# First slab's norm ahead, a four-tile opening for slabs 0 and 1, and a middle stage placed two places earlier

## The chip, the cores and the metric

The kernel runs on one core of one Trainium2 chip. The metric is the device time of one execution in microseconds (us), as a median of several runs. Engines are named as the profile names them: PE (TensorE, matmuls; PEld is its weight loads), DVE (VectorE), ACT (ScalarE), POOL (GpSimd) and SP (SyncE, which here only issues DMAs). ACT and POOL issue some DMAs too.

## The reference

```
x = A_x                                    # (1, 2048, 640), bf16
xn = layernorm(x)                          # over the 640 columns, eps 1e-5
s = irfft2(rfft2(xn) * (w_r + 1j * w_i))   # over rows and columns, s in bf16
g = silu((gelu(xn @ w_gate) * (xn @ w_up)) @ w_down)    # 640 -> 1536 -> 640, Gelu by its tanh form
return x + s * g
```

## The kernel before, in words

The 2048 rows are cut into 16 **slabs** of 128 rows (X[:, n1, :], 640 columns each). Two branches are worked on at once.

The feed-forward branch takes the slabs in four groups of four (g = 0 to 3). A slab is normalized in place (`norm`, L218), turned by five PE transposes or a DMA transpose into XG, and then multiplied with the weights: for each of 12 weight **tiles** of 128 columns (t), five matmuls with Wg into the PSUM bank psg and five with Wu into psu (`ffn_piece`, L832; one of the two for all four slabs, 512 columns, is a "half tile"). ACT takes the Gelu of psg (L837), DVE multiplies it with psu into UT (L839). Then the down projection follows, either plainly (`down_third`, L967) or, for groups 1 and 2, as 14 `product`s of six matmuls of 320 columns (L933) with DVE and ACT work between them (L937 copies, L947 sums, L870 and L867 Tanh and Silu, L875 leftovers of the Tanh form, L907 sums of parts).

The spectral branch is a chain of small matrix products. Its first stage writes ZDR to DRAM. The **middle stage** reads it back as B (`load_B2`, L603) and runs in steps (`s2_step`, L681): step b puts px(b) on PE (L628), then pu(b-1) (L657); DVE begins the sort of pu(b-1) (L672); ACT copies px(b) to xs (L640) and DVE multiplies that with the spectral weights W1 and W2 (L644); ACT ends the sort (L672, two copies) and, every other step, SP stores the result to UDR. px and pu take turns in the two buffers of the pool psB, so pu needs the sort of the pu before it finished. The **inverse stage** loads UDR (`load_V`), transforms slab by slab (L735, L762, with ACT copies L737 and L763), and `finish` multiplies, adds x and stores.

The order is written by hand. `back` (L1000) is the list of PE's feed-forward pieces in order, one **place** each; `plan[s]` holds what is emitted behind place s, filled by `put(s, ...)`. Each engine runs its own instructions in that order. Group 0 takes places 0 to 35 and begins, while weights still arrive, with narrower pieces: slab 0 alone on tiles 0 and 1, slab 1 alone on them, slabs 0 and 1 together (256 columns) on tiles 2 to 7, then slabs 2 and 3 together on tiles 0 to 7. Places 60 to 71 and 96 to 107 hold the products of groups 1 and 2, one or two in each; other places hold a half tile or a third of a plain down projection. The middle stage's first step stands behind place `sb` = 67 (L1111), its later ones at sb + 3, 5, 7 and so on, and everything of the inverse stage counts on from there.

Loads: SP issues x slab by slab, Wu, and later tiles of both weights (L94 to L106); ACT issues Wg's tiles 0 to 5, two tiles to a load (L231). A load with two tiles reads rows of 512 bytes. A DMA whose turn among eight semaphores is still taken waits on its issuing engine.

The opening: PE runs 21 **warm-up** matmuls of 256 columns on ones (L588). DVE takes the statistics of a slab in two halves of 320 columns (`bn_half`, L189) and joins them (`bn_join`, L195). The root is taken for slab 0 by ACT (`root_act`, L214, behind which the Gelu table is loaded, L215), for later slabs by DVE (L205, adding epsilon) and POOL (L207, a power). The order on DVE is: statistics of slab 0, first half of slab 1, second half of slab 1, join, epsilon (L205), then the norm of slab 0 in two column parts, 0 to 383 and 384 to 639 (`norm_parts`, L984). `slab_Tparts` (L988) transposes the two parts into psB and copies the first to XG by DVE, the second by ACT (L995).

Of the kernel before, what the change touches and what calls it, by code (L numbers as in the profile page):

```python
# [10 lines left out]
BF16 = mybir.dt.bfloat16  # L11
INT32 = mybir.dt.int32
ACT = mybir.ActivationFunctionType
ALU = mybir.AluOpType
P = 128
# [17 lines left out]
def kernel(  # L33
# [39 lines left out]
    with tc.manual_schedule():  # L73
        build(nc, locals())


def build(nc, env):
    consts, big, wts, work, psA, psB = (env[k] for k in ("consts", "big", "wts", "work", "psA", "psB"))
    ZDR, UDR, X, Wg, Wu, Wd, W1, W2 = (env[k] for k in ("ZDR", "UDR", "X", "Wg", "Wu", "Wd", "W1", "W2"))
    xv, outv, wgv, wuv = (env[k] for k in ("xv", "outv", "wgv", "wuv"))  # L80
    A_w_r, A_w_i, B_w_down = (env[k] for k in ("A_w_r", "A_w_i", "B_w_down"))

    def load_x(n0, n, eng=nc.sync):
        eng.dma_start(out=X[:, n0:n0 + n, :], in_=xv[:, n0:n0 + n, :])

    def load_w(k, t0, t1, eng=nc.sync):
        f0, f1 = t0 * P, t1 * P
        eng.dma_start(out=(Wg, Wu)[k][:, :, f0:f1], in_=(wgv, wuv)[k][:, :, f0:f1])

    def load_gu(t0, t1):  # L90
        for k in range(2):
            load_w(k, t0, t1)

    load_x(0, 1)  # L94
    load_x(1, 1)
    load_w(1, 0, 2)
    load_w(1, 2, 4)
    load_x(2, 1)
    load_w(1, 4, 6)
    load_x(3, 1)  # L100
    load_gu(6, 8)
    load_x(4, 4)
    load_gu(8, 12)
    load_x(8, 4)
# [32 lines left out]
    UT = consts.tile([P, NT, 512], BF16, name="UT")  # L137
# [8 lines left out]
    def slot(k, *shape):  # L146
        return XG[:, k, :].rearrange("p (a b) -> p a b", b=shape[-1])
# [25 lines left out]
    def c1(name, dt=FP32):  # L173
        return consts.tile([P, 1], dt, name=name)

    done = set()
    mva = {}
    rstd = {}
    rall = {}
    nmr = {}  # L180
    xnT = {}
# [4 lines left out]
    def bn_half(n1, k):  # L186
        if k == 0:
            st_n[n1] = work.tile([P, 2, nc.vector.BN_STATS_DIM], FP32, tag="st", bufs=3, name="st")
        nc.vector.bn_stats(out=st_n[n1][:, k, :], in_=X[:, n1, 320 * k:320 * k + 320])  # L189

    def bn_join(n1):
        g = n1 // 4
        if g not in mva:
            mva[g] = work.tile([P, 4, nc.vector.BN_AGGR_DIM], FP32, tag="mva", bufs=2, name=f"mva{g}")
        nc.vector.bn_aggr(out=mva[g][:, n1 % 4, :], in_=st_n[n1])  # L195
# [6 lines left out]
    def root(n0, n):  # L202
        m = mva[n0 // 4][:, n0 % 4:n0 % 4 + n, :]
        ve = work.tile([P, 4], FP32, tag="ve", name="ve")[:, 0:n]
        nc.vector.tensor_scalar(out=ve, in0=m[:, :, 1], scalar1=1e-5, scalar2=None, op0=ALU.add)  # L205
        r = work.tile([P, 4], FP32, tag="rst", bufs=4, name="rst")[:, 0:n]
        nc.gpsimd.tensor_tensor(out=r, in0=ve, in1=mhalf[:, 0:n], op=ALU.pow)  # L207
        rall[n0] = r
        for k in range(n):
            rstd[n0 + k] = r[:, k:k + 1]  # L210

    def root_act(n1):
        rstd[n1] = c1("rst0")
        nc.scalar.activation(out=rstd[n1], in_=mva[n1 // 4][:, n1 % 4, 1:2], func=ACT.Abs_reciprocal_sqrt, bias=eps)  # L214
        nc.scalar.activation(out=warm, in_=negpi, func=ACT.Gelu_apprx_tanh)  # L215

    def norm(n1, c0=0, c1_=D):
        nc.vector.tensor_scalar(out=X[:, n1, c0:c1_], in0=X[:, n1, c0:c1_], scalar1=mva[n1 // 4][:, n1 % 4, 0:1],  # L218
                                scalar2=rstd[n1], op0=ALU.subtract, op1=ALU.mult)
        if c1_ == D:  # L220
            done.add(("n", n1))
# [6 lines left out]
    eps = c1("eps")  # L228
    nc.vector.memset(eps, 1e-5)
    nc.scalar.activation(out=warm, in_=eps, func=ACT.Abs_reciprocal_sqrt)  # L230
    for t in (0, 2, 4):  # L231
        load_w(0, t, t + 2, nc.scalar)
    b_0, b_1 = c1("b_0"), c1("b_1")
    nc.vector.memset(b_0, 320.0)
    nc.vector.memset(b_1, 0.0)
# [92 lines left out]
    stats(0)  # L328
    bn_half(1, 0)
    root_act(0)  # L330

    def tinv_phase(h):
# [251 lines left out]
    def warm_pe(n):  # L584
        if not warm_bank:
            warm_bank.append(bank(0))
        for _ in range(n):
            nc.tensor.matmul(warm_bank[0][:, 0:256], lhsT=ones[:, 0:P], rhs=ones, start=True, stop=True)  # L588
# [230 lines left out]
    def bank(k):  # L819
        return psA.tile([P, 512], FP32, tag="gu"[k], name="ps" + "gu"[k])  # L820

    cur = {}

    ges = {}

    def ffn_piece(g, t, k, c0, c1_):
        for j in range(c0 // P, c1_ // P):
            assert ("T", 4 * g + j) in done
        ps = bank(k)[:, c0:c1_]
        WT = (Wg, Wu)[k]  # L830
        for c in range(5):
            nc.tensor.matmul(ps, lhsT=WT[:, c, t * P:(t + 1) * P], rhs=xnT[g][:, c, c0:c1_],  # L832
                             start=(c == 0), stop=(c == 4))
        flush()
        if k == 0:
            ges[t] = work.tile([P, 512], BF16, tag="ge", bufs=3, name="ge")[:, c0:c1_]
            nc.scalar.activation(out=ges[t], in_=ps, func=ACT.Gelu_apprx_tanh)  # L837
        else:
            nc.vector.tensor_tensor(out=UT[:, t, c0:c1_], in0=ps, in1=ges[t], op=ALU.mult)  # L839

    def ffn_part(g, t, h):
        for k in range(2):
            ffn_piece(g, t, k, h * 256, h * 256 + 256)

    def ffn_half(g, t, k):
        ffn_piece(g, t, k, 0, 512)
# [8 lines left out]
    def flush():  # L855
        now = put_off[:]
        del put_off[:]
        for f in now:
            f()
# [109 lines left out]
            if t == NT - 1:  # L969
                gated(g, j, k, ph)  # L970

    def ffn_slab(j, tk):
        for t, k in tk:
            ffn_piece(0, t, k, j * P, j * P + P)

    GG, UU = ((0, 0), (1, 0)), ((0, 1), (1, 1))

    def run(*items):
        for it in items:
            it[0](*it[1:])  # L980

    PARTS = ((0, 3), (3, 5))

    def norm_parts(n1):  # L984
        for a, b in PARTS:
            norm(n1, a * P, b * P)

    def slab_Tparts(n1):  # L988
        if n1 == 0:
            xnT[0] = slot(0, 5, 512)  # L990
        for (a, b), ev in zip(PARTS, (nc.vector.tensor_copy, nc.scalar.copy)):
            pt = psB.tile([P, 5, P], BF16, tag="b")
            for c in range(a, b):
                nc.tensor.transpose(out=pt[:, c, :], in_=X[:, n1, c * P:(c + 1) * P], identity=ident)  # L994
            ev(out=xnT[0][:, a:b, n1 * P:n1 * P + P], in_=pt[:, a:b, :])  # L995
        done.add(("T", n1))

    NP = 8
    STR = (1, 2)
    back = [(run, (ffn_slab, 0, GG), (norm_parts, 1), (slab_Tparts, 1), (vt_iota, 1), (ffn_slab, 0, UU),  # L1000
             (inv_consts, 0), (inv_consts, 1)),
            (run, (ffn_slab, 1, GG + UU), (stats, 2), (root, 2, 1))]
    for h in range(2):
        for t in range(0 if h else 2, NP):
            back.append((ffn_part, 0, t, h))
        if h == 0:
            back[-1] = (run, (ffn_piece, 0, NP - 1, 0, 0, 256), (slab_Tparts, 3), (ffn_piece, 0, NP - 1, 1, 0, 256))
    for g in range(4):
        for t in range(NP if g == 0 else 0, NT):
            for k in range(2):  # L1010
# [10 lines left out]
    def put(s, *item):  # L1021
        plan[s].append(item)

    put(1, inv_rest)
    put(2, norm, 2)
    put(3, bn_half, 3, 0)
    put(4, bn_half, 3, 1)
    put(4, bn_join, 3)
    put(4, root, 3, 1)
    put(4, slab_T, 2, 1)  # L1030
    put(5, norm, 3)
    for g in range(5):
        put(3 + g, ft_v, g)
        put(8 + g, ft_v, 5 + g)
# [73 lines left out]
    put(z_end, load_B2)  # L1108
    for k in range(2):
        put(TURN + k, mg_turn, k)  # L1110
    sb = 67  # L1111
    AT = (0, 3, 5, 7, 9, 11, 13, 15, 17, 19, 21)
    for b in range(len(BURSTS)):
        put(sb + AT[b], s2_step, b)
# [9 lines left out]
    for i, (n0, n) in enumerate(DG):  # L1124
        a = vs0 + 6 * i
# [3 lines left out]
        d = a + (7 if n == 3 else 4)  # L1129
# [3 lines left out]
        for k in range(n):  # L1133
            put(min(d + 8 + k, LAST), finish, n0 + k)

    warm_pe(21)
    bn_half(1, 1)
    bn_join(1)
    root(1, 1)
    norm_parts(0)  # L1140
    slab_Tparts(0)
    warm_pe(2)

    put(5, phase_const)

# [35 lines left out]
```

## Time and profile before

| what | us |
|---|---|
| three runs: median (lowest to highest) | 193.76 (193.47 to 193.83) |
| the profiled execution's own time | 193.65 |
| its span (first to last instruction) | 191.9 |
| PE busy | 186.1 |
| DVE busy | 150.9 |
| ACT busy | 131.9 |
| POOL busy | 53.9 |
| slab 0 landed; slab 1 landed | 3.10; 4.36 |
| norm of slab 0 begins; first transpose; first real matmul | 5.62; 6.05; 6.84 |
| last matmul begins | 188.44 |

All clock readings in this document count from the span's start, those of one profiled execution. Durations of matmuls are modelled ends: the distance from one start to the next tells the pace. The 1.75 us between the span and the execution's own time lie outside what the trace shows.

### The profile page before, as it was taken

The numbers are of one execution on the slowest core, as the hardware profiler recorded it, in microseconds if no ns is written. First come the engines' busy times: TensorE is split into PE (matmuls) and PEld (weight loads), VectorE is DVE, ScalarE is ACT, GpSimd is POOL, SyncE is SP. The second block draws the span as 40 slices with busy tenths as digits, with TensorE's granted clock in tenths as the row PEclk, the third lists the DMA queues.
The fourth block names the chain that finished last, engine by engine and source line by source line (L and its number), as shares of the span: only waits on it lengthen the run. The fifth ranks groups of instructions, "written<-read, shape, count | busy, mean of one in ns | idle before, by whom it ended". The sixth has DMA issues, their size and how long they took to land.

```text
span 191.9 us, 4068 instructions
## 1 busy us (share of the span) xinstructions
PE 186.1 (97%) x1453; PEld 115.6 (60%) x1469; DVE 150.9 (79%) x364; ACT 131.9 (69%) x241; POOL 53.9 (28%) x91
## 2 busy tenths in 40 slices
PE   7999999999999999999999999999999999999993
PEld 5788854677655665566543334347775555556772
DVE  6787889899799889846978677685445898888973
ACT  4658557957878778536697878634989776876622
POOL 4458768999040200000000000002030134150400
PEclk9999999999999999999999999999999999999999
DMA  6999999948889994249996444149900084778842
GB/s 164 300 329 360 370 332 170 172 99 318 178 165 191 211 300 120 78 111 230 223 108 123 106 103 103 42 107 273 266 5 0 0 117 111 152 153 213 121 174 62
DMA packets 39700, 32.43 MB, mean 169 GB/s; under 512 B 12928, under 2 KB 37760, under 8 KB 39552
## 3 DMA queue, kind: packets, MB, share of 16 engines
q1 hardware_dynamic: 35888, 27.91, 58.6%
q0 software_dynamic: 1824, 3.28, 9.4%
q10 hardware_dynamic: 1968, 0.98, 1.9%
q8 instruction: 11, 0.18, 0.4%
q14 instruction: 9, 0.07, 0.1%
HBM read 19.03 MB, written 7.88 MB: 140 GB/s over the span
## 4 chain that ended last, share of the span: by engine, by line
PE 95%; DMA 2%; DVE 1%; issue 1%; SPq 0%; ACT 0%
PE psu L832 27%; PE psg L832 27%; PE psg L967 7%; PE psg L933 7%; PE psu L967 6%; PE psu L933 5%; PE pu L657 2%; PE pd L762 2%; PE pv L735 2%; PE pz L555 2%; PE pd L573 2%; PE px L628 2%; DMA X<-in_A_x_dram 2%; PE pt L994 1%; PE pd L575 1%
## 5 line engine op out<-in xcount | busy, mean ns | idle before, releaser
L832 PE MATMUL psu<-XG,Wu 128*128 128x512 bf16 (+2 forms) x284 | 60.4, 342 | 0.5 <-issue 0.3
L832 PE MATMUL psg<-XG,Wg 128*128 128x512 bf16 (+2 forms) x280 | 60.1, 341 | 0.6
L839 DVE TENSOR_TENSOR UT<-psu,ge 128x512 bf16<-128x512 f32 (+2 forms) x58 | 34.4, 594 | 13.6 <-PE psu L832 8.1
L837 ACT ACTIVATE ge<-psg 128x512 bf16<-128x512 f32 (+2 forms) x58 | 30.3, 523 | 21.3 <-PE psg L832 20.6
L832 PEld LDWEIGHTS <-Wu 128*128 128x128 bf16 x290 | 25.9, 98 | 20.9 <-issue 3.4
L832 PEld LDWEIGHTS <-Wg 128*128 128x128 bf16 x290 | 26.5, 98 | 18.8 <-issue 0.2
L967 PEld LDWEIGHTS <-UT 128*128 128x128 bf16 x204 | 19.1, 98 | 6.9
L813 POOL DMA_DIRECT2D VY<-in_A_x_dram x12 | 10.6, 964 | 26.2 <-ACT W L737 10.5
L713 POOL COPY vr<-VY 128x128 bf16<-128x128 bf16 x2 | 0.6, 291 | 60.2 <-DMA VY<-UDR 60.2
L644 DVE TENSOR_TENSOR RZ<-xs,W 128x960 bf16<-128x960 bf16 (+2 forms) x22 | 13.3, 647 | 4.4 <-ACT xs L640 4.4
L967 PE MATMUL psg<-Wd,UT 128*128 128x320 bf16 (+1 forms) x108 | 15.7, 290 | 0.0
L578 ACT CAST RZ<-pd 128x660 bf16<-128x660 f32 x16 | 11.3, 706 | 5.2 <-PE pd L575 5.2
L189 DVE BATCH_NORM_STATS2 st<-X 128x6 f32<-128x320 bf16 x32 | 14.0, 476 | 0.6 <-DMA X<-in_A_x_dram 0.4
L933 PEld LDWEIGHTS <-UT 128*128 128x128 bf16 x120 | 11.4, 98 | 4.8 <-issue 0.4
L967 PE MATMUL psu<-Wd,UT 128*128 128x320 bf16 (+1 forms) x96 | 13.9, 293 | 0.0
L737 ACT CAST W<-pv 128x640 bf16<-128x640 f32 x16 | 11.1, 691 | 3.1 <-PE pv L735 3.1
L763 ACT ACTIVATE W<-pd 128x640 bf16<-128x640 f32 x16 | 11.3, 706 | 1.5 <-PE pd L762 1.5
L557 ACT CAST GEN<-pz 128x640 bf16<-128x640 f32 x16 | 11.2, 698 | 1.2 <-PE pz L555 1.2
L672 ACT CAST RX<-pu 128x480 bf16<-128x480 f32 (+3 forms) x22 | 10.8, 489 | 1.1 <-DVE RX L672 0.3
L640 ACT CAST xs<-px 128x960 bf16<-128x960 f32 (+2 forms) x11 | 10.3, 933 | 0.0
L207 POOL TENSOR_TENSOR rst<-ve,mhalf 128x1 f32<-128x1 f32 (+1 forms) x6 | 5.5, 913 | 11.5 <-DVE ve L205 11.5
L933 PE MATMUL psg<-X,UT 128*128 128x320 bf16 x48 | 7.8, 300 | 0.0
(202 smaller groups left out, 302.1 us busy)
## 6 DMA issues: line engine op xcount, KB each, us to landing
ZDR<-RZ SPq DMA_DIRECT2D x16, 160.5 KB, 4.1
UDR<-RX SPq DMA_DIRECT2D x10, 240.8 KB, 3.1
B<-ZDR SPq DMA_DIRECT2D x8, 240.8 KB, 5.2
W<-UDR SPq DMA_DIRECT2D x2, 963.0 KB, 9.1
X<-in_A_x_dram SPq DMA_DIRECT2D x3, 640.0 KB, 10.3
Wd<-in_B_w_down_dram SPq DMA_DIRECT2D x1, 1920.0 KB, 14.6
VY<-in_A_x_dram POOLq DMA_DIRECT2D x12, 160.0 KB, 4.3
out_dram<-VY SPq DMA_DIRECT2D x12, 160.0 KB, 2.8
```

What stands on the lines that cost most here:

```text
L189: nc.vector.bn_stats(out=st_n[n1][:, k, :], in_=X[:, n1, 320 * k:320 * k + 320])
L557: nc.scalar.copy(out=Zt[n1], in_=pz)
L578: nc.scalar.copy(out=zd.rearrange("p c (q e) -> p c q e", e=10), in_=pd[:, :, 0:330].rearrange("p c (e q) -> p c q e", q=33))
L644: nc.vector.tensor_tensor(out=pp[-1], in0=xs, in1=WT[:, :, h0:h0 + n, l0:l0 + w], op=ALU.mult)
L672: copy(out=out, in_=src)
L737: nc.scalar.copy(out=vs, in_=pv)
L763: nc.scalar.activation(out=parts(eobuf, i, 5)[:, :, n1 - DG[i][0], :], in_=pd, func=ACT.Copy, scale=(2.0 if n1 // 4 in BY_SILU else 1.0) / ...
L832: nc.tensor.matmul(ps, lhsT=WT[:, c, t * P:(t + 1) * P], rhs=xnT[g][:, c, c0:c1_], start=(c == 0), stop=(c == 4))
L837: nc.scalar.activation(out=ges[t], in_=ps, func=ACT.Gelu_apprx_tanh)
L839: nc.vector.tensor_tensor(out=UT[:, t, c0:c1_], in0=ps, in1=ges[t], op=ALU.mult)
L933: nc.tensor.matmul(ps, lhsT=lhs[:, t, :], rhs=rhs[:, t, :], start=(t == 0 and i in (0, 1, 3)), stop=(t == 5), skip_group_check=i in (2, 4, ...
L967: nc.tensor.matmul(ph, lhsT=UT[:, t, j * P:(j + 1) * P], rhs=Wd[:, t, c0:c1_], start=(t == 0), stop=(t == NT - 1))
```

## The change

- Behind the warm-up matmuls (18 now, with four more after slab 0's transposes, for 21 and two), the norm and the transposes of slab 0 are emitted ahead of the second half of slab 1's statistics. Slab 1's root is taken by ACT as slab 0's is, and the Gelu table is loaded behind both.
- Slabs 0 and 1 alone are multiplied with tiles 0 to 3 (`ffn_quad`): four tiles of 128 columns share one PSUM bank, the first three row blocks of the weights for all four tiles, then the last two. One Gelu and one product of 512 columns follow (`multi_out`). Slabs 0 and 1 together then do tiles 4 to 7, two tiles to a bank (`ffn_multi`), and so do slabs 2 and 3 on tiles 0 to 7. Both copies of slab 1's and slab 0's transposes are DVE's.
- The first weights come as two row parts of four tiles each, Wg's on ACT's queue and Wu's on SP's; tiles 4 to 7 follow on SP in one load per weight. All rows of weights are then 1024 bytes.
- Statistics, norms and transposes of slabs 2 and 3 and the inverse constants move to other places; the list `back` keeps its length.
- `sb` goes from 67 to 65.

```diff
+    def load_w(k, t0, t1, eng=nc.sync, c0=0, c1_=5):
         f0, f1 = t0 * P, t1 * P
+        eng.dma_start(out=(Wg, Wu)[k][:, c0:c1_, f0:f1], in_=(wgv, wuv)[k][:, c0:c1_, f0:f1])
...
+    PARTS = ((0, 3), (3, 5))
     load_x(0, 1)
     load_x(1, 1)
-    load_w(1, 0, 2)
-    load_w(1, 2, 4)
+    for part in PARTS:
+        load_w(1, 0, 4, nc.sync, *part)
     load_x(2, 1)
-    load_w(1, 4, 6)
+    load_w(0, 4, 8)
     load_x(3, 1)
-    load_gu(6, 8)
+    load_w(1, 4, 8)
...
-    for t in (0, 2, 4):
-        load_w(0, t, t + 2, nc.scalar)
+    for part in PARTS:
+        load_w(0, 0, 4, nc.scalar, *part)
...
+    def ffn_quad(k, j, *part):
+        assert ("T", j) in done
+        if part[0] == 0:
+            cur["m"] = bank(k)
+        ps = cur["m"].rearrange("p (t w) -> p t w", w=P)
+        WT = (Wg, Wu)[k]
+        for a, b in [PARTS[i] for i in part]:
+            for i in range(4):
+                for c in range(a, b):
+                    nc.tensor.matmul(ps[:, i, :], lhsT=WT[:, c, i * P:(i + 1) * P],
+                                     rhs=xnT[0][:, c, j * P:(j + 1) * P], start=(i + c == 0), stop=(c == 4),
+                                     skip_group_check=True)
+        if part[-1] == 1:
+            multi_out(k, 0, ps, j * P, j * P + P)
+    def ffn_multi(k, t0, n, c0, c1_, half=None):
...
+        for i in range(n) if half is None else range(half * n // 2, (half + 1) * n // 2):
+            for c in range(5):
+                nc.tensor.matmul(ps[:, i, :], lhsT=WT[:, c, (t0 + i) * P:(t0 + i + 1) * P], rhs=xnT[0][:, c, c0:c1_],
+                                 start=(c == 0), stop=(c == 4))
...
-        for (a, b), ev in zip(PARTS, (nc.vector.tensor_copy, nc.scalar.copy)):
+        for (a, b), ev in zip(PARTS, (nc.vector.tensor_copy, nc.scalar.copy if n1 > 1 else nc.vector.tensor_copy)):
...
-    back = [(run, (ffn_slab, 0, GG), (norm_parts, 1), (slab_Tparts, 1), (vt_iota, 1), (ffn_slab, 0, UU),
-             (inv_consts, 0), (inv_consts, 1)),
-            (run, (ffn_slab, 1, GG + UU), (stats, 2), (root, 2, 1))]
...
+    back = [(run, (ffn_quad, 0, 0, 0, 1), (vt_iota, 1)),
+            (run, (ffn_quad, 1, 0, 0), (slab_Tparts, 1), (ffn_quad, 1, 0, 1)),
+            (ffn_quad, 0, 1, 0, 1),
+            (ffn_quad, 1, 1, 0, 1)]
+    for h, k, t0 in ((0, 0, 4), (0, 0, 6), (0, 1, 4), (0, 1, 6)) + tuple((1, k, t) for t in (0, 2, 4, 6) for k in range(2)):
+        back.append((ffn_multi, k, t0, 2, 256 * h, 256 * h + 256))
+    back[6] = (run, (ffn_multi, 1, 4, 2, 0, 256, 0), (slab_T, 2, 1), (ffn_multi, 1, 4, 2, 0, 256, 1))
+    back[7] = (run, (ffn_multi, 1, 6, 2, 0, 256, 0), (slab_Tparts, 3), (ffn_multi, 1, 6, 2, 0, 256, 1))
...
-    put(1, inv_rest)
-    put(2, norm, 2)
-    put(3, bn_half, 3, 0)
-    put(4, bn_half, 3, 1)
-    put(4, bn_join, 3)
-    put(4, root, 3, 1)
-    put(4, slab_T, 2, 1)
-    put(5, norm, 3)
+    put(1, stats, 2)
+    put(1, root, 2, 1)
+    put(2, bn_half, 3, 0)
+    put(2, bn_half, 3, 1)
+    put(3, norm, 2)
+    put(3, bn_join, 3)
+    put(3, root, 3, 1)
+    put(3, inv_consts, 0)
+    put(3, inv_consts, 1)
+    put(4, inv_rest)
+    put(5, norm_parts, 3)
...
-    sb = 67
+    sb = 65
...
-    warm_pe(21)
+    warm_pe(18)
+    norm_parts(0)
+    slab_Tparts(0)
+    warm_pe(4)
     bn_half(1, 1)
     bn_join(1)
-    root(1, 1)
-    norm_parts(0)
-    slab_Tparts(0)
-    warm_pe(2)
+    root_act(1)
+    gelu_table()
+    norm_parts(1)
```

More of the change, by code (lines that the diff above doesn't have):

```diff
@@ L84, in load_x @@
         eng.dma_start(out=X[:, n0:n0 + n, :], in_=xv[:, n0:n0 + n, :])
-    def load_w(k, t0, t1, eng=nc.sync):
+    def load_w(k, t0, t1, eng=nc.sync, c0=0, c1_=5):
         f0, f1 = t0 * P, t1 * P
-        eng.dma_start(out=(Wg, Wu)[k][:, :, f0:f1], in_=(wgv, wuv)[k][:, :, f0:f1])
+        eng.dma_start(out=(Wg, Wu)[k][:, c0:c1_, f0:f1], in_=(wgv, wuv)[k][:, c0:c1_, f0:f1])
     def load_gu(t0, t1):
@@ L212, in root_act, with gelu_table @@
     def root_act(n1):
-        rstd[n1] = c1("rst0")
+        rstd[n1] = c1("rst%d" % n1)
         nc.scalar.activation(out=rstd[n1], in_=mva[n1 // 4][:, n1 % 4, 1:2], func=ACT.Abs_reciprocal_sqrt, bias=eps)
+    def gelu_table():
         nc.scalar.activation(out=warm, in_=negpi, func=ACT.Gelu_apprx_tanh)
@@ L839, in ffn_piece, with multi_out @@
             nc.vector.tensor_tensor(out=UT[:, t, c0:c1_], in0=ps, in1=ges[t], op=ALU.mult)
-    def ffn_part(g, t, h):
-        for k in range(2):
-            ffn_piece(g, t, k, h * 256, h * 256 + 256)
+    def ffn_quad(k, j, *part):
[13 more added lines that the diff above has]
+    def ffn_multi(k, t0, n, c0, c1_, half=None):
+        w = c1_ - c0
+        for j in range(c0 // P, c1_ // P):
+            assert ("T", j) in done
+        if half in (None, 0):
+            cur["m"] = bank(k)[:, 0:n * w].rearrange("p (t w) -> p t w", w=w)
+        ps = cur["m"]
+        WT = (Wg, Wu)[k]
+        for i in range(n) if half is None else range(half * n // 2, (half + 1) * n // 2):
+            for c in range(5):
+                nc.tensor.matmul(ps[:, i, :], lhsT=WT[:, c, (t0 + i) * P:(t0 + i + 1) * P], rhs=xnT[0][:, c, c0:c1_],
+                                 start=(c == 0), stop=(c == 4))
+        if half != 0:
+            multi_out(k, t0, ps, c0, c1_)
+    def multi_out(k, t0, ps, c0, c1_):
+        n, w = 512 // (c1_ - c0), c1_ - c0
+        flush()
+        if k == 0:
+            ge = work.tile([P, 512], BF16, tag="ge", bufs=3, name="ge")[:, 0:n * w].rearrange("p (t w) -> p t w", w=w)
+            ges[t0, c0] = ge
+            nc.scalar.activation(out=ge, in_=ps, func=ACT.Gelu_apprx_tanh)
+        else:
+            nc.vector.tensor_tensor(out=UT[:, t0:t0 + n, c0:c1_], in0=ps, in1=ges[t0, c0], op=ALU.mult)
     def ffn_half(g, t, k):
@@ L970, in down_third @@
                 gated(g, j, k, ph)
[L972 to L976, printed above, removed]
     def run(*items):
@@ L980, in run @@
             it[0](*it[1:])
-    PARTS = ((0, 3), (3, 5))
     def norm_parts(n1):
@@ L999, in build @@
     STR = (1, 2)
-    back = [(run, (ffn_slab, 0, GG), (norm_parts, 1), (slab_Tparts, 1), (vt_iota, 1), (ffn_slab, 0, UU),
-             (inv_consts, 0), (inv_consts, 1)),
-            (run, (ffn_slab, 1, GG + UU), (stats, 2), (root, 2, 1))]
[L1003 to L1007, printed above, removed]
+    back = [(run, (ffn_quad, 0, 0, 0, 1), (vt_iota, 1)),
[6 more added lines that the diff above has]
+    back[7] = (run, (ffn_multi, 1, 6, 2, 0, 256, 0), (slab_Tparts, 3), (ffn_multi, 1, 6, 2, 0, 256, 1))
     for g in range(4):
```

## The prediction

> **What bounds the kernel now.** I read the page first, its busy shares and its chain of waits.
>
> ```profile
> PE 186.1 (97%) x1453; PEld 115.6 (60%) x1469; DVE 150.9 (79%) x364; ACT 131.9 (69%) x241; POOL 53.9 (28%) x91
> PE 95%; DMA 2%; DVE 1%; issue 1%; SPq 0%; ACT 0%
> ```
>
> TensorE (PE) works 186.1 of 191.9 us and carries 95% of the chain. From the first real matmul on it hardly stops, so only three things can move the end: when it starts, how much it has to do, and new waits on it. Second I read the chain over the first 7 us (start, length, what).
>
> ```profile
> 1.17 3.19 DMA X<-in_A_x_dram
> ...
> 4.38 0.90 DVE st L189 x2
> ...
> 5.30 0.22 DVE mva L195
> ...
> 5.55 0.15 DVE ve L205
> 5.70 0.30 DVE X L218
> ...
> 6.05 0.54 PE pt L994 x5
> ...
> 6.84 0.22 PE psg L832
> ```
>
> This is what the change aims at: the norm of slab 0 (L218) stands on DVE behind the statistics of slab 1, which wait for slab 1's load. Real matmuls begin at 6.84.
>
> **The start.** In the timeline slab 1's halves of statistics start at 4.38 and 4.79 and the norm at 5.62. The changed order keeps the first half ahead of the norm and puts the second behind it. So the norm takes the second half's place, 4.80 (its root on ACT is ready at 4.29+0.29 = 4.58): 0.82 sooner. The transposes follow the norm's start by 6.05-5.62 = 0.43, so 5.23.
>
> Here PE is still slow. The 21 warm-up matmuls are 0.213 apart, later ones of the same size 0.109; the pace changed after the last of them, which starts at 5.42 (the granted-clock row says full throughout; the spacing tells it). Eighteen warm-ups end at 1.18+18x0.213 = 5.02, so PE idles 0.2, and transposes at the slow pace cost about 0.15 more until the third is done. The copy then starts at 5.76 (0.26 behind the third's start, plus 0.07), takes 0.36, and 0.05 later the first matmul comes: 6.17 for 6.84, **-0.67**. The four warm-ups behind the transposes fill 5.60 to 6.03, inside that copy: nothing.
>
> The second part's copy moves from ACT to DVE and queues behind the first: done at 6.39, needed after 12 matmuls of 0.056, at 6.84. Nothing.
>
> Slab 1 now: second half 6.37, join 6.88, root on ACT 7.13 to 7.42, norm 7.46, transposes possible at 7.89. PE gets there after 32 matmuls, 7.96. Both copies on DVE: the first ends at 8.69 (+0.05 to PE), PE has its next use at 7.96+0.28+8x0.056 = 8.69. **+0.05**.
>
> The Gelu table load now stands behind that root on ACT (7.45 to 8.73, 1.28 by its row, plus 0.20). Behind it queue the four-tile Gelus, and for the first of these DVE's product. It runs 8.93 to 9.45; PE needs that PSUM bank back at about 10.97. Hidden by 1.5; without this cover it would cost what is over.
>
> **The work.** Slabs 0 and 1 on four tiles: 20 matmuls of 256 columns (0.109) become 40 of 128 (0.0557): 2.18 to 2.23, **+0.05**. The wider Gelus and products (523 and 594 ns for 512 columns, 277 and 292 for 128) save on ACT and DVE, off the path. There PE reaches slab 2's transposes at 13.7 and slab 3's at 15.1; by the new DVE order, norm 2 ends at 13.2 and slab 3's transposes can start at 14.6. Nothing.
>
> The inverse constants (5 of 0.06 on DVE) and their six POOL operations go from 11.8 to about 14.1, so POOL's next big operation starts 0.6 later. POOL's next wait, for DVE at 25.27, has 2.57 idle before it: hidden.
>
> **The weights.** PE now asks for all of tiles 0 to 3 in its first four groups: Wg's second row part at 6.84, Wu's at 8.24, then tiles 4 to 7 of Wg at 10.97 and of Wu at 13.15. Before, Wg 0-1 landed at 5.5, Wu 2-3 at 8.8, and the last of tiles 0 to 7 at 8.85+5.4 = 14.2. So what counts is the rate; the DMA view over 6 to 11 and over 13 to 20 us:
>
> ```profile
> DMA packets 2671, 1.51 MB, mean 301 GB/s; under 512 B 95, under 2 KB 2671, under 8 KB 2671
> DMA packets 1680, 2.59 MB, mean 370 GB/s; under 512 B 64, under 2 KB 1446, under 8 KB 1678
> ```
>
> The first window holds the two-tile loads (rows of 512 B), the second mostly rows of 1024 B and more. All weights come in rows of 1024 B now, so I take something near the second. Counting 0.22 MB until 3.0, then 340 GB/s, and 0.4 us to land: Wg's second part (1.38 MB with all ahead of it) 6.8, Wu's (1.64) 7.6, Wg 4-7 (2.46) 10.0, Wu 4-7 (3.28) 12.4. All in time, the first barely. **0**, from 0 to +1.05 (rival 1).
>
> [...]
>
> **The middle stage, two places sooner.** Each step of it puts px (in) and pu (out of the step before) on PE. The timeline of before:
>
> ```profile
> 92.48 0.40 PE L628 MATMUL px<-B,MG 64*64 64x161 bf16 x5
> ...
> 93.51 0.94 ACT L640 CAST xs<-px 128x966 bf16<-128x966 f32 x1
> ...
> 94.16 0.35 DVE L672 CAST RX<-pu 128x192 bf16<-128x192 f32 x1
> 94.49 1.24 DVE L644 TENSOR_TENSOR RZ<-xs,W 128x966 bf16<-128x966 bf16 x2
> 94.54 1.03 ACT L672 CAST RX<-pu 128x480 bf16<-128x480 f32 x2
> ...
> 96.27 0.58 PE L657 MATMUL pu<-RZ,N 64*64 64x161 bf16 x10
> ```
>
> From px to the next pu PE has 3.79 us, the chain over ACT and DVE needs 3.25. Two places sooner, steps 1 and 2 are parted by two products (0.81 each) where two products and a half tile (1.08) stood. On the clock of before: px of step 1 at 90.85, pu of step 2's place at 93.57. ACT's xs goes 91.48 to 92.45, DVE (behind the first step's products and three Tanh leftovers) sorts 92.48 to 92.83, ACT's sorts end at 93.90, and only then is pu's bank free: 93.95. **+0.38** (0 to +0.5). One step on, before itself loses time: pu at 99.35 takes 0.74 where the others take 0.58, since L644 ends late. With the new spacing that product is ready ahead of PE: **-0.2**.
>
> Step 0's px moves from 89.60 to 87.97. Its two loads land at 86.55 and 87.6 (83.49+4.1); 0.35 to spare. The inverse stage moves with it: ten transforms share ACT with twelve products; going through its new order the banks come back in time but for one: **+0.06**. More PE work lies between the V loads and their first use than before. At the end PE, last Silu, product, sum and store stand as they did.
>
> **Sum.** -0.67+0.05+0.05+0+0.38-0.2+0.06 = **-0.33**. The profiled execution took 193.65 (span 191.9 and 1.75 around it), 0.11 under the median of 193.76. 193.65-0.33 = **193.3**. Measurement can tell 0.2% (0.39 us) from no change, so the forecast lies at that edge.
>
> **Rivals.**
> 0. *Nothing given back*: the order on ACT and DVE turns out kinder, pu waits for nothing: -0.67+0.10-0.2, 192.9. For it: the 0.38 is a sum of seven hand-offs.
> 1. *Weights late*: 512 or 1024 B makes no difference; then Wu 4-7 lands 13.6 to 14.2 for 13.15 and Wg's second part 0.4 late: +0.45 to +1.05, 194.05 at the middle. Against it: the 370.
> 2. *Slower: PE's pace.* The pace changed after 4.3 us of unbroken warm-up; now only 3.84 us come before a gap. If the gap puts the change off by as long as the warm-up's remainder and the transposes, to 8.9, the real work from 6.17 runs at half pace for 2.7 us and loses 1.4: 194.7. It decides as soon as the pace changes after 7.0 (half of the 0.83 from 6.17 eats the forecast); for it to end slower by 0.2%, after 7.6. Against it: the gap is 0.2, and before had one of 0.32 without harm. [...]
> 3. *B late*: if step 0's loads come 0.8 later than they do against PE, +0.5: 193.8.
> 4. *It doesn't do what it says*: the norm still waits for slab 1's load; if that lands 0.6 later among longer weight packets, the start gains nothing: 193.9.
>
> **Chances.** Forecast 0.43 (193.0 to 193.6; half of it beyond 0.2%), rival 0 0.20, rival 1 0.15, rival 2 0.09, rival 3 0.07, rival 4 0.06. Faster: 0.22+0.20 = 0.42. Slower: rival 2 and about half of rival 1 and a third of the last two, 0.20. Within 0.2%: 0.38. The range takes in all but rival 2 and the fringe of rival 0: 192.7 to 194.2.
>
> **What would show it.** First four-tile matmul at 6.2; the matmul pace full by 6.0; no PE idle ahead of the second row parts or of tiles 4 to 7; weights at over 340 GB/s until 12; pu of step 1 waiting about 0.4 and none at the third; slab 2's transposes at 13.7. Wrong, if the first matmul is not before 6.5, or if PE waits for weights.

## The result, and the profile after

The changed kernel takes 194.22 us (median of 22 runs, 193.71 to 195.22) against 193.52 for the kernel before, run beside it. The ratio is 1.0032, 95% interval 1.0023 to 1.0040: slower by 0.3%, where 193.3 and a small gain had been forecast. The ratios are worked out from the fast runs and not from the two medians, so they can differ a little from the medians' ratio.

The page of the changed kernel, busy times and shares of the chain:

```profile
PE 185.3 (96%) x1472; PEld 115.7 (60%) x1488; DVE 151.0 (78%) x358; ACT 130.0 (68%) x230; POOL 52.9 (27%) x90
...
PE 92%; DMA 3%; ACT 1%; issue 1%; DVE 1%
```

PE still carries the chain, but 3% is now DMA. The chain over the first 18 us (start, length, what) says which:

```profile
0.72 0.91 ACT L234
1.63 0.04 issue
1.67 6.07 DMA Wg<-in_B_w_gate_dram
7.73 0.05 issue
7.78 0.62 PE psg L854 x8
...
9.07 0.28 PE pt L1027 x5
...
12.08 2.20 PE psg L870 x20
...
14.30 0.60 ACT ge L881
14.90 0.38 ACT GEN L365
15.28 0.59 ACT XG L551
15.87 0.29 issue
16.16 0.69 DVE UT L883
16.85 0.28 DVE XG L1028
17.12 0.04 issue
17.17 0.93 PE psg L870 x7
```

The norm of slab 0 has left the chain, as meant. Its place is taken by the load of Wg's second row part, which lands at 7.73. A second detour follows: DVE's copy of slab 3's transposes (L1028) stands behind its product of tiles 4 and 5 (L883), and PE's work on slabs 2 and 3 waits for that copy. (The chain's way from there back over ACT is inferred; what held the product until 16.16 is taken up below.)

PE's timeline shows the first stop. The bracket is idle time and what ended it:

```profile
5.92 0.83 PE L854 MATMUL psg<-XG,Wg 128*128 128x128 bf16 x12
7.78 0.62 PE L854 MATMUL psg<-XG,Wg 128*128 128x128 bf16 x8 [1.02 <-DMA Wg<-in_B_w_gate_dram]
```

PE starts 0.92 sooner than before (5.92 for 6.84), does the 12 matmuls of the first row part, and stands. From start to start the step is 1.24 where 0.056 is the pace: 1.19 lost.

Where the time went, from the two profiled executions (194.64 and 193.65, 0.99 apart, where the medians are 0.70 apart; the rows are rounded):

| stretch | forecast | measured |
|---|---|---|
| start of the first real matmul | -0.67 | -0.92 |
| wait for Wg's second row part | 0 | +1.19 |
| wait for slab 3's copy | 0 | +0.33 |
| rest of the opening (work, copies) | +0.10 | +0.06 |
| middle and inverse stage | +0.24 | -0.09 |
| last landing to the span's end | not in the sum | +0.07 |
| outside the span | taken as constant | +0.34 |
| sum | -0.33 | +0.98 |

The opening ends where slabs 2 and 3 begin on tile 0: 17.17 for 16.50. From there to the last matmul it is 171.84 for 171.93. Over all runs (22 to 32 each) the medians say the same in milder numbers: span 192.2 for 191.8 or 191.9, outside it 2.00 for 1.78. Each round of experiments was timed beside the kernel before, so times of different rounds are best compared by their ratios to it.

### The profile page after: what moved, and what is told of

Its sections match the earlier page's. It is cut to its first block, busy times and chain, and to the rows that moved or that the text cites. A ratio compares the mean times of both kernels' runs of the same rounds, so it can differ in the third digit from the quotient of the medians.

```text
span 192.5 us, 4072 instructions
## 1 busy us (share of the span) xinstructions
PE 185.3 (96%) x1472; PEld 115.7 (60%) x1488; DVE 151.0 (78%) x358; ACT 130.0 (68%) x230; POOL 52.9 (27%) x90
## 4 chain that ended last, share of the span: by engine, by line
PE 92%; DMA 3%; ACT 1%; issue 1%; DVE 1%
PE psu L836 23%; PE psg L836 22%; PE psg L1007 7%; PE psg L973 7%; PE psu L1007 6%; PE psu L973 5%; PE psg L870 3%; DMA Wg<-in_B_w_gate_dram 3%; PE pu L661 2%; PE pv L739 2%; PE pd L766 2%; PE pz L559 2%; PE psu L870 2%; PE pd L577 2%; PE px L632 2%; PE psu L854 1%
## 5 line engine op out<-in xcount | busy, mean ns | idle before, releaser
L836 PE MATMUL psu<-XG,Wu 128*128 128x512 bf16 x194 | 49.0, 379 | 0.5 <-issue 0.3
L836 PE MATMUL psg<-XG,Wg 128*128 128x512 bf16 x190 | 48.7, 379 | 0.5
L843 DVE TENSOR_TENSOR UT<-psu,ge 128x512 bf16<-128x512 f32 x40 | 27.5, 688 | 11.3 <-PE psu L836 6.8
L841 ACT ACTIVATE ge<-psg 128x512 bf16<-128x512 f32 x40 | 23.9, 596 | 16.0 <-PE psg L836 15.2
L836 PEld LDWEIGHTS <-Wu 128*128 128x128 bf16 x200 | 18.0, 98 | 20.2 <-issue 3.2
L836 PEld LDWEIGHTS <-Wg 128*128 128x128 bf16 x200 | 18.6, 98 | 18.0
L881 ACT ACTIVATE ge<-psg 128x512 bf16<-128x512 f32 x8 | 4.8, 597 | 7.1 <-PE psg L870 5.0
L209 POOL TENSOR_TENSOR rst<-ve,mhalf 128x4 f32<-128x4 f32 (+1 forms) x5 | 5.4, 1072 | 11.0 <-DVE ve L207 9.6
```

## The experiments

**Theory W**: the loss is Wg's second row part. Rivals: the earlier middle stage (M), slab 3's copy (P), the queue itself (Q). The first four kernels, two with one part alone and two with one part undone or mended:

one_queue:
```diff
-    for part in PARTS: load_w(1, 0, 4, nc.sync, *part)
+    for k in range(2):
+        for part in PARTS: load_w(k, 0, 4, nc.sync, *part)
...
-    for part in PARTS: load_w(0, 0, 4, nc.scalar, *part)
```


> The changed kernel with its first four weight loads all on SP's queue, in the order in which PE needs them (Wg's first and second row part, then Wu's), behind x of slabs 0 and 1. Theory W (the changed kernel lost because Wg's second row part, last on ACT's queue, landed at 7.73 for a need at 6.59): with 0.98 MB ahead of and with that part, 0.22 MB moved by 3.0 and 340 GB/s after, it lands at about 5.7; Wu's parts at 6.8 and 7.6 for needs at 7.03 and 8.0. PE then has no gap of over 0.2 us between its first real matmul (5.9) and slab 1's transposes, slabs 2 and 3 begin at 15.6 to 16.0 (17.17 in the changed kernel, 16.50 before), and the time is 192.9 (192.6 to 193.2). Rival M (the middle stage two places sooner is what costs): the opening gains, the middle gives it back, 193.5 or more. Rival P (the copy of slab 3 behind DVE's product is what costs as well): a gap of 0.3 ahead of slabs 2 and 3 stays, 193.2. Rival Q (one queue is slower than two at this point): Wg's second part lands after 7, and the time is 194 or more.

after_sb67: `sb = 65` back to `sb = 67` in the changed kernel.

> The changed kernel with the middle stage and the inverse stage back at place 67. Theory W: the middle stage is worth little either way, 194.2 give or take 0.2, and the first wait of pu, 0.15 us in the changed kernel, goes while the waits of px and pu at the third step, 0.3 before, come back. Rival M (the earlier middle stage costs 0.4 or more): 193.8 or less.

before_sb65: `sb = 67` to `sb = 65` in the kernel before.

> The kernel before with only the middle and the inverse stage moved to place 65. Theory W: 193.5 give or take 0.2, no change that can be told. Rival M: 193.9 or more. The prediction's own sum (+0.38-0.2+0.06) would give 193.8.

before_norm_first, on the kernel before:
```diff
-    warm_pe(21)
+    warm_pe(18)
+    norm_parts(0)
+    slab_Tparts(0)
+    warm_pe(4)
     bn_half(1, 1)
     bn_join(1)
-    root(1, 1)
-    norm_parts(0)
-    slab_Tparts(0)
-    warm_pe(2)
+    root_act(1)
+    gelu_table()
```


> The kernel before with only the start changed: 18 warm-up matmuls, norm and transposes of slab 0 ahead of the second half of slab 1's statistics, four more warm-ups, slab 1's root on ACT and the Gelu table behind it; weights, tiles and places as before. Theory W (what counts in the opening is when weights land): the first real matmul comes at 5.9 to 6.2, but Wg's tiles 4 and 5 land at 11.37 and were needed at 11.58, so 0.2 us of the start is kept at most, and 193.3 follows (193.2 to 193.5). Rival: the earlier start is kept in full, 192.6 to 192.9.

| kernel | us | ratio to before (95%) | first matmul | slabs 2+3 begin | last matmul |
|---|---|---|---|---|---|
| one_queue | 194.07 | 1.0020 (1.0005 to 1.0036) | 6.06 | 17.11 | 188.94 |
| after_sb67 | 194.49 | 1.0045 (1.0030 to 1.0059) | 6.30 | 16.67 | 188.61 |
| before_sb65 | 193.90 | 1.0011 (0.9998 to 1.0025) | 6.60 | | 188.10 |
| before_norm_first | 194.30 | 1.0038 (1.0024 to 1.0052) | 6.23 | | 189.43 |

By their times the two kernels that move the middle stage alone do not settle rival M. after_sb67 expected 194.2 give or take 0.2 and got 194.49; before_sb65 expected 193.5 and got 193.90, the rival's own number. The stretches in the profiles decide. From the first matmul of the pz stage to the last matmul of all, the kernels with place 67 take 146.96 and 146.97 (before, after_sb67), those with 65 take 146.87, 146.86, 146.87 (after, one_queue, before_sb65). So the earlier middle stage gains 0.09, everything lost is lost ahead of it or behind it, and rival M falls. What before_sb65 lost stands behind the last matmul (*before_turn*, below); the rest of after_sb67's loss stays open.

Theory W in its simple form falls too: one_queue expected 192.9 and got 194.07. The waits of PE until 17.5 in it (who waits for what: us in total, times, longest):

```profile
PE psu L853 <- DMA Wu<-in_B_w_up_dram: 0.6, 2, 0.4
PE psg L869 <- DVE XG L1027: 0.2, 1, 0.2
```

The wait at Wg is gone, but now Wu's parts come late (7.79 and 9.13 for needs at 7.3 and 8.8). From 3.0 to 4.0 its one queue moved 115 KB, where the changed kernel's two moved 340. Rival Q had the time right, but not the landing: Wg's second part came at 6.75, not after 7. Nor is one queue slow as such: in weights_small (third round) SP's queue moved 300 KB from 3.5 to 4.5 with hardly a packet on the other. What held it back here stays open.

before_norm_first is *slower* by 0.7, which neither side expected. Two of its waits:

```profile
7.62 0.54 PE L996 MATMUL pt<-ident,X 128*128 128x128 bf16 x5 [0.67 <-DVE X L220]
...
8.88 0.93 PE L834 MATMUL psg<-XG,Wg 128*128 128x128 bf16 x9 [0.16 <-ACT ge L839]
```

The first is the larger: ten matmuls of slab 0 are not enough to cover slab 1's norm, whose statistics and root now stand behind slab 0's norm, and PE's step there is 0.89 from start to start, where 0.056 is the pace. Then ACT's Gelu table load (1.28, at 7.17) stands behind slab 1's root, so the Gelus that free the PSUM banks and ACT's copy of slab 1's transposes wait until 8.57 and 8.89; PE's steps there are 0.38 and 0.32. In the changed kernel PE has 32 matmuls ahead of slab 1's transposes, DVE does that copy, and the first Gelu has slack, so these waits do not appear.

**Second round: which order of loads, and slab 3's copy.**

copy_ahead: the product of tiles 4 and 5 is emitted behind slab 3's transposes.
```diff
-    back[6] = (..., (slab_T, 2, 1), (ffn_multi, 1, 4, 2, 0, 256, 1))
-    back[7] = (..., (slab_Tparts, 3), (ffn_multi, 1, 6, 2, 0, 256, 1))
+    back[6] = (..., (slab_T, 2, 1), (ffn_multi, 1, 4, 2, 0, 256, 1, True))
+    back[7] = (..., (slab_Tparts, 3), (multi_late,), (ffn_multi, 1, 6, 2, 0, 256, 1))
```


> The changed kernel with DVE's product of tiles 4 and 5 (slabs 0 and 1) behind its copy of slab 3's transposes instead of ahead of it. In the runs so far with the changed order, PE goes 0.42 to 0.44 us from one matmul to the next ahead of slabs 2 and 3 where 0.11 is its pace. Theory P (that copy, queued behind the product, is 0.3 of the loss): the step falls to under 0.2, the products move back by under 0.5, and the time falls by 0.2 to 0.35 against the changed kernel: 193.9. Rival (the product, late itself, then holds the PSUM bank that the next psu needs): the 0.3 comes back one group later, 194.2.

part_swap:
```diff
-    for part in PARTS: load_w(1, 0, 4, nc.sync, *part)
+    load_w(0, 0, 4, nc.sync, *PARTS[1])
+    load_w(1, 0, 4, nc.sync, *PARTS[1])
...
-    for part in PARTS: load_w(0, 0, 4, nc.scalar, *part)
+    for k in range(2): load_w(k, 0, 4, nc.scalar, *PARTS[0])
```


> The changed kernel with Wg's second row part on SP's queue ahead of Wu's second, and Wu's first on ACT's queue behind Wg's first. Theory O (two queues are served alike while both have work, so a load lands by its place in its queue, and about 0.17 to 0.19 MB come in every half microsecond): Wg's second part lands at 6.0 to 6.6 (7.25 to 7.73 in the runs so far), Wu's first at 7.2 to 7.7, so the wait of 0.4 to 1.2 at Wg's second part goes, and one of 0.2 to 0.6 at Wu's first, needed at 7.0, takes its place. Time 193.6 to 194.0. Rival T (the last load of ACT's queue is late whatever it is, as SP has more queued behind): Wu's first lands at 7.7, and the time stays at 194.2 or goes over.

gates_first: part_swap, and
```diff
-    (run, (ffn_quad, 1, 0, 0), (slab_Tparts, 1), (ffn_quad, 1, 0, 1)), (ffn_quad, 0, 1, 0, 1),
+    (run, (slab_Tparts, 1), (ffn_quad, 0, 1, 0, 1)), (ffn_quad, 1, 0, 0, 1),
```


> As part_swap, and PE takes slab 1's transposes and its Wg groups ahead of both Wu groups; the second copy of slab 0 is ACT's as in the kernel before, so that slab 1's norm comes about 0.25 sooner (transposes at about 7.2). Theory O: Wu is now needed at about 8.5 and all its parts have landed by 8.0; PE waits 0.1 to 0.3 for slab 1's transposes and for no weight; slabs 2 and 3 begin at about 16.1 (0.3 of it the copy of slab 3), 0.4 sooner than in the kernel before, and the middle stage gains 0.1 more: 193.3 (193.1 to 193.6). If the opening is not what decides: 194 or more.

gates_copy: gates_first and copy_ahead together.

> gates_first and copy_ahead in one. Theories O and P together: slabs 2 and 3 begin at about 15.8 against 16.50 in the kernel before, 193.0 (192.8 to 193.3), faster than the kernel before by 0.2 to 0.4%. If the order of the copy does not matter: as gates_first.

| kernel | us | ratio (95%) | median span | outside it |
|---|---|---|---|---|
| changed kernel | 194.22 | 1.0032 (1.0023 to 1.0040) | 192.2 | 2.00 |
| copy_ahead | 194.25 | 1.0032 (1.0018 to 1.0046) | 191.9 | 2.35 |
| part_swap | 194.64 | 1.0036 (1.0019 to 1.0054) | 192.7 | 2.00 |
| gates_first | 194.45 | 1.0034 (1.0020 to 1.0048) | 192.2 | 2.36 |
| gates_copy | 194.04 | 1.0025 (1.0005 to 1.0045) | 192.1 | 1.99 |

All four missed their expected times (193.9, 193.6 to 194.0, 193.3 and 193.0). copy_ahead's time is that of its rival, but its profile is not: its step ahead of slabs 2 and 3 is 0.11, PE's pace, for 0.44, and its median span is 0.3 shorter, as theory P asked. The gain is lost outside the span, 2.35 for 2.00, which no theory had thought of. The column "outside" (the execution's own time less its span) must have a cause of its own.

part_swap shows Wg's second part at 6.85 and Wu's first at 7.32, in its profiled execution (193.58, one of its fastest; the median is 194.64); its twelve spans run from 191.6 to 193.2, so other executions presumably had later landings, which their records do not show. In gates_first and gates_copy the same load landed at 7.33 and 6.87. Moving parts between two queues that both stay full settles nothing.

**Third round: is it the weights at all, and what lies outside the span?**

weights_small: loads of row block 0 alone first (`load_w(k, 0, 4, eng, 0, 1)`), blocks 1 to 4 behind tiles 4 to 7, and in `ffn_quad`
```diff
-                    nc.tensor.matmul(ps[:, i, :], lhsT=WT[:, c, i * P:(i + 1) * P],
+                    nc.tensor.matmul(ps[:, i, :], lhsT=WT[:, 0, i * P:(i + 1) * P],
```


> The changed kernel with the four-tile groups reading the first row block of their weights five times over, so that 0.13 MB of each weight are enough to begin; the other four row blocks of tiles 0 to 3 come behind tiles 4 to 7. It leaves out the true products of slabs 0 and 1 with tiles 0 to 3; every instruction of PE, DVE and ACT and all bytes stay. Theory D (four tiles for one slab ask for 1.31 MB in the 2.2 us of 40 matmuls, 590 GB/s, where 350 arrive): with that demand gone PE waits for no weight, slabs 2 and 3 begin at 15.7 to 16.0 (17.17 in the changed kernel's profile), and the time is 193.2 (193.0 to 193.5), 0.2 of which lies outside the span. Rival (something else in the opening, such as slab 1's norm or the pace of PE, sets it): 193.9 or more.

pad:
```diff
+    for k in range(20): put(40 + k // 2, pad_act, k)        # nc.scalar.copy(out=pad[:, k:k + 1], in_=negpi)
+    for k in range(13): put(40 + k // 2, pad_dve, 20 + k)   # nc.vector.tensor_copy, likewise
```


> The changed kernel with 20 one-column copies more on ACT and 13 more on DVE (places 40 to 49), results unused: 337 and 461 instructions as in the kernel before (336 and 461) for 317 and 448. Theory F (the last 8 KB blocks of ACT's and DVE's instructions are fetched behind the program's end in the changed kernel, at 193.7 and 194.5, where the kernel before had them at 176.5 and 186.6): both fetches come before the end, what lies outside the span falls from 2.0 to about 1.78, and the time to 194.0; the span stays. Rival (what lies outside the span has nothing to do with these fetches): it stays at 2.0.

before_turn:
```diff
-    load_x(12, 4)
+    load_x(12, 2)
+    load_x(14, 2)
```


> The kernel before with the load of slabs 12 to 15 as two loads, so that 121 DMAs take turns at the eight semaphores instead of 120, and the last store has the first in SP's closing list of waits instead of the last. Theory E (behind the last landing SP goes through the rest of that list at 0.06 us each): the span's end follows the last landing by 1.35 instead of 0.91, and the time is 0.4 longer, 194.0. Rival (the list costs nothing, as waits already met are free): 193.6.

front_two, on the kernel before (with the start of before_norm_first, and `norm_parts(1)` behind it):
```diff
     load_w(1, 0, 2)
+    load_w(0, 2, 4)
     load_w(1, 2, 4)
     load_x(2, 1)
-    load_w(1, 4, 6)
+    load_gu(4, 6)
...
-    for t in (0, 2, 4): load_w(0, t, t + 2, nc.scalar)
+    load_w(0, 0, 2, nc.scalar)
...
-    back = [(run, (ffn_slab, 0, GG), (norm_parts, 1), (slab_Tparts, 1), (vt_iota, 1), (ffn_slab, 0, UU),
+    back = [(run, (ffn_slab, 0, GG), (up_late, 0), (up_late, 1), (slab_Tparts, 1), (vt_iota, 1), (up_out,),
```


> The kernel before with norms of slabs 0 and 1 as early as in the changed kernel, and its two-tile opening kept: slab 0 on tiles 0 and 1 with Wg and Wu, then slab 1's transposes, then slab 1. Wg 0-1 alone on ACT's queue; SP's brings Wu 0-1, Wg 2-3, Wu 2-3, x of slab 2, Wg 4-5, Wu 4-5. It asks for 0.66 MB in the 1.1 us of slab 0's 20 matmuls and then for no more until about 8.8. Theory D: Wu 0-1 lands at 6.1 for a need at 6.5, the only wait is about 0.4 for slab 1's transposes at 7.4, slabs 2 and 3 begin at 15.9 to 16.2 (16.50 before): 193.0 (192.8 to 193.3). Rival (its 512-byte rows, 300 GB/s, are late at tiles 4 to 7, as in the kernel before they landed only 0.2 ahead of their need): 193.4 or more.

| kernel | us | ratio (95%) | median span | outside it |
|---|---|---|---|---|
| weights_small | 193.38 | 0.9988 (0.9977 to 0.9999) | 191.55 | 1.83 |
| pad | 194.06 | 1.0022 (1.0013 to 1.0032) | 192.3 | 1.78 |
| before_turn | 194.10 | 1.0023 (1.0014 to 1.0031) | 192.3 | 1.80 |
| front_two | 194.28 | 1.0030 (1.0020 to 1.0040) | 192.5 | 1.77 |

*weights_small*: with the weights' demand taken away, and all instructions and bytes kept, the time falls by 0.84 to 193.38, PE runs from 5.37 without a stop to slab 3's copy, and slabs 2 and 3 begin at 15.89. Of the 0.84, about 0.65 is in the span and 0.17 outside it (one instruction block fetched behind the end, for two; see *pad*). That the weights' lateness is the bulk of the loss is shown.

*pad*: the instruction blocks. The DMA view of the changed kernel from 191.6 to 196, all of it but the first microsecond behind the program's end at 192.5, has one queue:

```profile
q14 instruction: 2, 0.02, 1.1%
```

Two blocks of 8 KB of instructions come at 193.66 and 194.54. In the kernel before, the last two come at 176.45 and 186.60, and this window has no packet at all. With 20 and 13 more instructions on ACT and DVE the two fetches are back at 176.13 and 185.98, the window from 191.6 is empty:

```profile
DMA packets 0, 0.00 MB, mean 0 GB/s; under 512 B 0, under 2 KB 0, under 8 KB 0
```

and the time outside falls from 2.00 to 1.78, just as expected. Over all kernels of this study: no fetch behind the end, 1.75 to 1.80; one, 1.79 to 1.91; two, 1.99 to 2.36. The changed kernel pays 0.2 us (0.34 in its profiled execution) for having *fewer* instructions on ACT and DVE. Why two fetches cost 2.00 in three kernels and 2.35 in copy_ahead and gates_first stays open. The time outside the span is thus no constant here: it runs from 1.75 to 2.36, a spread of 0.61 where a gain of 0.33 had been forecast.

*before_turn*: SP's closing list. The span of the kernel before ends 0.91 after its last store lands; with 121 DMAs, 1.34 after it. The last store now has the first of the eight semaphores, and SP goes through the other seven waits behind it, one every 0.06 us, from 190.79 to 191.22. The time rises by 0.5. before_sb65 has 121 DMAs too (1.35): its last matmul came 0.34 sooner, and the list takes 0.44 back. The changed kernel has 119 and pays 0.07.

*front_two* missed (193.0 expected): Wu 0-1 landed at 6.66, later than asked but ahead of its first use at 6.76; the same table load (at 7.09) again held two Gelus and ACT's copy until 8.50 and 8.81. PE's steps there are 0.94 and 0.32. A two-tile opening needs its Gelus early; the four-tile one does not.

**Fourth round: order against rate, and the sum.** loads_ordered keeps ACT's queue to one load, so that nothing which is needed later shares with what is needed next:
```diff
     load_x(1, 1)
+    load_w(0, 0, 4, nc.sync, *PARTS[1])
     for part in PARTS: load_w(1, 0, 4, nc.sync, *part)
...
-    for part in PARTS: load_w(0, 0, 4, nc.scalar, *part)
+    load_w(0, 0, 4, nc.scalar, *PARTS[0])
```


> The changed kernel with Wg's first row part alone on ACT's queue, and on SP's, behind x of slab 1, what PE needs next, in that order: Wg's second part, Wu's first, Wu's second. Theory O (order: later bytes were moved first): from x of slab 1's landing at 4.3 on, with 0.36 MB in a microsecond and 0.5 us to land, Wg's second part lands at 5.8 (7.25 to 7.73 in the changed kernel), Wu's first at 6.9, its second at 7.6; no wait for weights over 0.2 us, slabs 2 and 3 begin at 15.9 to 16.2 (0.33 of it slab 3's copy), and the time is 193.5 (193.2 to 193.8). Rival R (rate: 1.64 MB can not be in by 7.7 in any order): Wg's second part is early but Wu's parts come after 7.7 and 8.6, PE waits 0.6 or more there, and the time is 194 or more.

all_mended: loads_ordered with the edits of copy_ahead, pad and before_turn.

> loads_ordered, and the product of tiles 4 and 5 behind slab 3's copy, 20 and 13 unused one-column copies on ACT and DVE (so that the last instruction blocks are fetched before the end), and the load of slabs 12 to 15 in two (120 DMAs, the last store last in SP's closing list, as in the kernel before). If the four causes add up: against loads_ordered 0.3 less by the copy, 0.2 by the fetches, 0.06 by the list; slabs 2 and 3 begin at 15.6 to 15.9, and the time is 192.9 (192.6 to 193.2), faster than the kernel before by 0.2 to 0.5%. If the opening's gain is given back later: 193.4 or more.

loads_ordered: 193.41, ratio 0.9982 (0.9968 to 0.9995). Wg's second part lands at 6.31, Wu's at 7.37 and 8.10, and slabs 2 and 3 begin at 16.35, just above the expected 16.2. PE's waits until 17.5 are one, and its weight loads (PEld) have one for a weight, at the first real matmul:

```profile
PE psg L870 <- DVE XG L1028: 0.2, 1, 0.2
...
6.18 1.12 PEld L854 LDWEIGHTS <-Wg 128*128 128x128 bf16 x20 [0.25 <-DMA Wg<-in_B_w_gate_dram]
```

Wg's first part, alone on ACT's queue beside a full one, lands at 6.14 here (5.20 in the changed kernel). DVE's copy that the same matmul needs ended at 6.06, so this costs under 0.1.

all_mended: 193.14, ratio 0.9968 (0.9953 to 0.9983), 0.3% faster than the kernel before. The four loads land at 5.61, 5.84, 6.94 and 7.92, slabs 2 and 3 begin at 15.80, outside the span are 1.77 us. Over the first 18 us its chain holds nothing but PE from the first warm-up on; it begins:

```profile
1.17 4.02 PE psg L593 x18
5.20 0.53 PE pt L1036 x5
5.73 0.51 PE psg L593 x4
6.24 1.12 PE psg L855 x20
7.36 0.67 PE psu L855 x12
8.03 0.28 PE pt L1036 x5
8.31 0.45 PE psu L855 x8
```

Rival R (the rate) falls: the same bytes in another order are in time, or at most 0.1 late. Both kernels came out within their expected ranges. By its time the order of the loads alone takes the kernel from 194.22 to 193.41 (about 0.1 of it outside the span, with one fetch there for two), and the four causes together to 193.14. Between the two, 0.27 of an expected 0.56 came out; with twelve runs each, whose spans spread over 0.5 and 0.7, the smaller causes are not told apart there.

## Why the prediction was wrong

**The weights** are the step that failed: "So what counts is the rate", with Wg's second part landing at 6.8 and a cost of 0. It landed at 7.73 and cost 1.19. The rate was foretold rightly. In the window 6 to 11 us the changed kernel moves

```profile
DMA packets 1762, 1.78 MB, mean 356 GB/s; under 512 B 90, under 2 KB 1762, under 8 KB 1762
```

where the kernel before had 301: rows of 1024 B came faster here, and rival 1's reason (row length makes no difference) did not happen. The number of queues is not the reason: front_two, whose weights come in rows of 512 B and on SP's queue alone in this window, has 301 as well. But I counted the bytes "ahead of" each load as if one line served them all. There are two lines. From 4.9 to 6.4, SP's queue, with Wu's parts, x of slab 2 and tiles 4 to 7 behind it, moved 290 KB and ACT's 241 KB. By 7.0, 1.63 MB had moved, 0.25 MB more than my count for Wg's second part, and that part was still not complete: its last packets went one in 0.09 us from 6.5 to 7.1, each taking 0.046, and the landing followed 0.6 later (0.4 in my sum). So from 4.9 to 6.4 SP's queue, with much waiting, took over half of what moved from a load that was needed at once (290 against 241 KB), and that load's tail went at one packet in about two packet times. The split was not the same throughout: from 4.5 to 5.0 SP's queue moved 159 KB and ACT's 24. That the later bytes on the other queue are the cause is shown by loads_ordered; how the two queues share in each moment is not. The prediction weighed the row length and not the second queue. A second check was in the numbers as well: 1.31 MB asked for in 40 matmuls of 0.0557 is 590 GB/s, against the 356 of this window.

The range of this step, 0 to +1.05, had a lateness in it, and "wrong, if PE waits for weights" named it; its measure was +1.19. Rival 1's 194.05 came near the 194.22 by luck: its reason did not happen. The size varies, too. In three other profiled executions with the same opening and loads (after_sb67, copy_ahead, pad) the part landed at 7.25, 8.49 and 7.73, and PE lost 0.33, 1.46 and 0.38.

**Slabs 2 and 3, "Nothing"**, failed as well. The transposes were ready as forecast in their order, but the copy behind them was not traced through DVE's queue: the product of tiles 4 and 5 stands ahead of it. +0.33, removed by the new order in copy_ahead and all_mended (step 0.11). The product itself starts 0.47 to 0.48 after the matmuls it reads are done (16.16 for 15.67, by DVE's own wait, in the changed kernel; one_queue and after_sb67 alike); what holds it that long stays open.

**The start**: the mechanism was right, the size was off. -0.92 for -0.67, because PE's pace turned full at 3.9 in this execution, not at 5.5. That was luck: in after_sb67, copy_ahead and pad the first real matmul came at 6.30, 6.38 and 6.58, where 6.17 was forecast. The gain was worth nothing in any case, as PE then stood until the weights had landed. Rival 2 did not happen here, but the pad kernel's profiled execution ran at half pace until 6.9, past its first real matmuls.

**The work**: the 523 and 594 ns given for Gelus and products of 512 columns are means over three widths. At 512 columns alone they take 597 and 687 in the kernel before, still less than four narrow ones (277 and 292 each).

**The middle stage**: +0.38 was +0.15. From px of the second step, DVE's sort comes at +1.36, not at +1.63 as I had it, so ACT's sorts and the bank follow 0.27 sooner:

```profile
91.52 0.41 PE L632 MATMUL px<-B,MG 64*64 64x161 bf16 x5
...
92.20 0.96 ACT L644 CAST xs<-px 128x966 bf16<-128x966 f32 x1
...
92.88 0.35 DVE L676 CAST RX<-pu 128x192 bf16<-128x192 f32 x1
...
93.27 1.03 ACT L676 CAST RX<-pu 128x480 bf16<-128x480 f32 x2
...
94.35 0.61 PE L661 MATMUL pu<-RZ,N 64*64 64x161 bf16 x10
```

The later gain of -0.2 was -0.24 (two steps on, px and pu together take 0.74 from 97.70, where before they took 0.98 from 99.04). Together -0.09, the number that all kernels with place 65 show. The inverse stage's +0.06 did not appear.

**Outside the sum**: the span's surroundings were taken as a constant 1.75. They were not: +0.2 by the instruction blocks, and +0.07 inside the span by SP's list. A chain of waits does not show them; at a difference of 0.3% they are more than a third of the result.

## What to carry to other kernels

When an opening is made to start sooner, write down for each load when its first use now comes, and let no queue move bytes needed later while one needed next is still under way. A rate that suffices in sum did not help here: at 356 GB/s, Wg's second part, beside SP's deep queue, landed at 7.73 where 6.8 had been counted. Follow each copy that PE waits for through its engine's whole order, not only to its operands. Below half a percent, compare the time outside the span and the last landing to the end first: the number of instructions and of DMAs alone moved these kernels by 0.2 to 0.5 us.

## What the runs showed of the hardware that was not expected

- Blocks of 8 KB of instructions are fetched behind the program's end in some kernels, and the execution pays for them outside the span: 1.75 to 1.80 us with none, 1.99 to 2.36 with two. 33 more instructions brought both fetches ahead of the end.
- Behind the last landing, each wait left in SP's closing list costs 0.06 us though it is already met; the seven of before_turn were worth 0.44.
- PE's pace turned from half to full between 3.9 and 6.9 us over the sixteen profiled executions, a spread of 3.0, though the warm-up began at 1.17 or 1.18 in every one. What sets the moment is not shown.
- Rows of 512 B came at 301 GB/s, on one queue as on two, and rows of 1024 B at 356 (windows from 6 to 11 us).
